# Recurrent attention and a two-way maxout layer: attention output in 64-column tiles, copied in the order it lies, token order restored by the stores

## The chip, the cores and the metric

The kernel runs on one core of one Trainium2 chip. The metric is the device time of one execution in microseconds. Times are told as medians of a few runs; a profiled execution, taken by the hardware profiler, gives the trace that the rows below come from. PE is the matrix engine (PEld its weight loads), DVE, ACT and POOL are the vector, scalar and general engines, and SP issues every DMA of this kernel, in the order of the program. Each core has 16 DMA engines, which share the packets of a transfer.

## What is computed

A recurrent attention over 768 tokens, for 4 batches and 8 heads of 48 columns, is followed by a layer that takes the larger of two products and multiplies once more:

```python
for t in range(S):
    cur = einsum('bhd,bhe->bhde', u[None] * kt, vt)
    y[:, :, t] = einsum('bhd,bhde->bhe', rt, state + cur)
    state = wt[:, :, :, None] * state + einsum('bhd,bhe->bhde', kt, vt)
x = y.transpose(0, 2, 1, 3).reshape(B * S, H * D)      # 3072 x 384
out = np.maximum(x @ w1, x @ w2) @ w_out               # d_ff 1024, out 3072 x 384
```

## The kernel before

Tokens go in segments of 256. A unit (`UNITS`) is one or two batches of one segment: the first four units hold one batch each of segment 0, the other four two batches each of segments 1 and 2. In a unit a token is numbered 2g + i: g runs over 128 partitions when the inputs are loaded (`load`, L357), and i over the two neighbours. After that g is split in two halves q of 64.

The text `ORDER` lists every step by name, unit and part, and the program is written out in that order; each engine runs its own share of it in that order, held by semaphores alone. There is no other scheduler. `name@a`, `@d`, `@p` put a step on ACT, DVE or POOL.

The steps that the change touches come at the end of a unit:

- `yi` (L654) adds the part of the output that comes from the state: for a head pair p and a half q, the weights are 128 rows (two heads of 64) by 96 columns (two heads of 48) of the state copy `S_b`, the moving operand is 128 tokens of `rT`. The output has heads' columns on partitions: pair p starts at row 96p of a 384-row range that is folded into blocks of 128 partitions.
- `ya` (L666) adds the part within a segment: for each head, 64 rows of masked scores `M` and 64 columns of `vp` (48 of them are the head's, the other 16 zero, so that the head's piece begins at a multiple of 32). It is called once per batch and neighbour j (in the first unit also once per half of the heads).
- `into` (L645) says which rows of the PSUM tile `Y` a matmul writes, and whether it is the first to write them; it keeps a set of the 32-row bands begun.
- `xe` (L678) copies `Y` to `xT` in bf16, on ACT for ten of twelve calls and on DVE for two.
- `gt` (L684) and `rl` (L696) multiply `xT` by the difference of the two first weights and keep the positive part in `gT`; `op` (L705) multiplies `xT` by a folded weight (L709) and `gT` by the last one (L713), with 128 tokens as the output's partitions.
- `oe` (L716) copies the 128 x 384 result to one of four `osb` buffers, and `os` (L721) stores it: 24 stores of 128 rows of 1,536 bytes, issued by SP between the loads and the transposes by DMA (`dt`, L566) of later units.

`Y` lies as q, block, i, g: the two neighbours i are 64 columns apart. Before, `xe` interleaves them, so that `xT`'s columns are tokens in their order, and the stores write 128 consecutive rows.

Of the kernel before, what the change touches and what calls it, by code (L numbers as in the profile page):

```python
# [114 lines left out]
def _body(tc, r, k, v, w, u, moe_w1, moe_w2, moe_w_out, out):  # L115
    nc = tc.nc
    B, H, S, D = r.shape
    P = 128
    Q = P // 2
    HD = H * D  # L120
    d_ff = moe_w1.shape[1]
    KO = HD // P
    FO = d_ff // P
    NP = H // 2
    DP = 64
# [11 lines left out]
    def wt_(shape, dt, tag, bufs=1):  # L137
        return wk.tile(shape, dt, tag=tag, name=tag, bufs=bufs)
# [19 lines left out]
    S_b = const.tile([P, 2, B, NP, 2, D], BF16)  # L158
# [6 lines left out]
    def copy(e, o, i):  # L165
        (nc.scalar.copy if e == "a" else nc.vector.tensor_copy if e == "d" else nc.gpsimd.tensor_copy)(  # L166
            o, i)
# [472 lines left out]
    def ytile(s, b):  # L640
        if b not in s.y:
            s.y[b] = pair()
        return s.y[b]

    def into(s, b, q, r0, n, i=None):  # L645

        o, c = r0 % P, r0 // P * P
        new = not all((b, q, x) in s.begun for x in range(o, o + n, 32))
        s.begun |= {(b, q, x) for x in range(o, o + n, 32)}
        y = ytile(s, b)[o:o + n, q, c:c + P].rearrange("c (i g) -> c i g", i=2)  # L650
        return dict(out=y if i is None else y[:, i, :], start=new, stop=False,
                    skip_group_check=True)

    def yi(s, b):  # L654
        for p in range(NP):
            for q in range(2):
                if s.c == 0 and q == 0:
                    continue
                for m in range(3):
                    nc.tensor.matmul(  # L660
                        lhsT=S_b[:, q, s.b0 + b, p].rearrange("d e c -> d (e c)")[
                            :, m * 32:(m + 1) * 32],
                        rhs=s.rT[:, b, :, p, q, :],
                        **into(s, b, q, p * 96 + m * 32, 32))

    def ya(s, b, j, y):  # L666
        n = NP // s.np
        for e in range(2):
            for p in range(y * n, (y + 1) * n):
                for m in range(2):  # L670
                    for q in range(2):
                        g = slice(q * Q, (q + 1) * Q)
                        nc.tensor.matmul(  # L673
                            lhsT=s.vp[g, b, 2 * p + e, j, m * 32:(m + 1) * 32],
                            rhs=s.M[b, j][g, :, 2 * p + e, :],
                            **into(s, b, q, p * 96 + (e + m) * 32, 32))

    def xe(s, b, e):  # L678
        if not hasattr(s, "xT"):
            s.xT = wt_([P, 4, KO, P], BF16, "xT", 2)  # L680
        copy(e, s.xT[:, 2 * b:2 * b + 2].rearrange("c q k (g i) -> c q k i g", i=2),
             s.y[b][:, :, 0:HD].rearrange("c q (k i g) -> c q k i g", i=2, k=KO))

    def gt(s, f):  # L684
        t = bank(F32, "G")
# [35 lines left out]
    def os(s, a):  # L721
        t = getattr(s, f"os{a}")
        t0 = (s.b0 + a // 2) * S + s.t0 + (a % 2) * P
        nc.sync.dma_start(out=out[t0:t0 + P, :], in_=t)

    ops = {"tri": c_tri, "tri2": c_tri2, "ident": c_ident, "mask": c_mask, "zero": c_zero, "u": dma_u,
           "wload": w_load, "woload": wo_load, "wdiff": w_diff, "hot": hot, "identb": c_identb, "identq": c_identq,
# [4 lines left out]
            "we": we, "rk": rk, "ru": ru, "dg": dg, "dd": dd, "di": di, "rw": rw, "kw": kw, "vb": vb,  # L732
            "scale": scale, "tr": tr, "te": te, "kv": kv, "st": st, "sm": sm, "sb": sb, "sc": sc,
            "mk": mk, "yi": yi, "ya": ya, "xe": xe, "gt": gt, "rl": rl, "op": op,
            "oe": oe, "os": os, "load": load, "dt": dt, "hi": hi, "lo": lo}
    for o in ORDER:
        o, _, e = o.partition("@")
        name, *a = o.split(".")
        a = [int(x) if x.isdigit() else x for x in a] + ([e] if e else [])
# [39 lines left out]
```

## Time and profile before

| what | value |
|---|---|
| median of 3 runs | 152.26 us (150.28 to 152.46) |
| profiled execution, its own time | 152.13 us |
| its span, from the first to the last instruction | 150.3 us |
| PE busy in the span | 92% |
| DVE / ACT / POOL busy | 79% / 61% / 60% |
| mean granted clock of PE | 0.974 |
| DMA queue of SP, share of 16 engines | 79.7% |
| the 24 stores, median from issue to landing | 2.5 us |

A row of a group reads: line, engine, operation, out<-in, partitions x elements and type, count, then busy us, mean ns of one, and the engine's idle time before it with what ended it. Matmuls overlap, so a group's busy time is the union of its records and is far below count times mean.

### The profile page before, as it was taken

The page shows a single profiled execution, that of the slowest core. Times are in us where ns is not written, and L with a number is a line of the kernel's source. Part 1 is how long each engine was busy: PE and PEld are TensorE (multiplying, and loading weights), DVE is VectorE, ACT ScalarE, POOL GpSimd, SP SyncE. Part 2 cuts the span into 40 slices and gives each one's busy share as a digit, 9 for nine tenths or more (in the row PEclk, how much of TensorE's full clock was granted, in tenths as well). Part 3 has the DMA queues.
Part 4 walks back from the last instruction along what each step waited for, and adds up shares of the span by engine and source line. Part 5 has one row for each costly group of instructions (what it writes and reads, how often), then busy time and mean ns, then how long its engine had stood idle before and what let it go on. Part 6 is the DMA issues. An engine that isn't in the chain of part 4 may idle for free.

```text
span 150.3 us, 5551 instructions
## 1 busy us (share of the span) xinstructions
PE 138.8 (92%) x2404; PEld 84.3 (56%) x2404; DVE 118.5 (79%) x161; ACT 91.6 (61%) x168; POOL 89.8 (60%) x102
## 2 busy tenths in 40 slices
PE   4779997799899998999999999999999999999991
PEld 1344645475676666764766546564667455664550
DVE  4593697999999999939999969796899887836510
ACT  3255463959989985995897785638736465033011
POOL 7878449796290779289999499590499900000000
PEclk9975899999999999999999999999999999999998
DMA  4999995999998959999993999679976693034042
GB/s 112 279 268 344 338 314 201 326 313 291 320 285 203 284 131 268 323 239 272 248 256 95 183 257 283 190 59 261 228 186 190 107 193 90 4 108 160 0 161 105
DMA packets 71187, 31.85 MB, mean 212 GB/s; under 512 B 66293, under 2 KB 70390, under 8 KB 71162
## 3 DMA queue, kind: packets, MB, share of 16 engines
q1 hardware_dynamic: 71162, 31.49, 79.7%
q8 instruction: 19, 0.31, 0.9%
q14 instruction: 6, 0.05, 0.1%
HBM read 23.61 MB, written 4.73 MB: 189 GB/s over the span
## 4 chain that ended last, share of the span: by engine, by line
PE 56%; DVE 18%; DMA 7%; POOL 6%; issue 5%; ACT 3%; SPq 3%; DVEq 0%; POOLq 0%; ACTq 0%
PE G L713 17%; PE G L691 16%; PE G L709 7%; DMA lr<-in_r_dram 7%; PE Y L673 4%; DVE M L635 3%; PE Y L626 3%; PE Y L660 2%; DVE dg L487 2%; PE G L232 2%; DVE rku L174 2%; SPq L357 2%; DVE kp L174 2%; DVE wst L398 2%; DVE rp L174 2%
## 5 line engine op out<-in xcount | busy, mean ns | idle before, releaser
L713 PE MATMUL G<-wo_sb,gT 128*128 128x384 bf16 x192 | 35.3, 326 | 0.1
L691 PE MATMUL G<-xT,wd_sb 128*128 128x256 bf16 (+1 forms) x192 | 34.1, 326 | 0.7 <-ACT xT L166 0.7
L635 DVE CAST_PREDICATED M<-mask,Y 128x1024 bf16<-128x1024 int32 (+1 forms) x26 | 28.9, 1136 | 4.1 <-PE Y L626 4.0
L701 ACT ACTIVATE gT<-G 128x512 bf16<-128x512 f32 x37 | 21.0, 603 | 11.1 <-PE G L691 11.0
L713 PEld LDWEIGHTS <-gT 128*128 128x128 bf16 x192 | 18.7, 98 | 12.9 <-ACT gT L701 0.7
L691 PEld LDWEIGHTS <-wd_sb 128*128 128x128 bf16 x192 | 18.2, 98 | 13.0 <-DVE M L501 0.7
L178 POOL TENSOR_TENSOR kp<-lk,iE 128x384 bf16<-128x384 f32 x16 | 18.2, 1163 | 3.0 <-ACT iE L445 2.2
L166 ACT COPY osb<-G 128x384 f32<-128x384 f32 x17 | 8.0, 481 | 14.2 <-PE G L713 13.4
L232 PE MATMUL G<-S_b 128*128 128x512 bf16 x48 | 14.8, 463 | 2.1 <-DVE S_b L261 2.1
L178 POOL TENSOR_TENSOR rku<-rku,u_b 128x384 f32<-128x384 f32 x14 | 14.1, 1029 | 3.2 <-DVE rku L174 2.0
L709 PE MATMUL G<-wc_sb,xT 128*128 128x384 bf16 x72 | 15.7, 328 | 0.0
L166 ACT CAST xT<-Y 128x768 bf16<-128x768 f32 x10 | 10.1, 1021 | 9.1 <-PE Y L660 7.5
L166 ACT COPY RK<-G 128x1024 bf16<-128x1024 bf16 x12 | 11.8, 1024 | 0.8 <-PE G L550 0.8
L487 DVE TENSOR_REDUCE dg<-rku 128x16 f32<-128x768 f32 x12 | 11.0, 945 | 0.0
L174 DVE TENSOR_TENSOR rp<-lr,G 128x768 bf16<-128x768 f32 (+2 forms) x13 | 10.5, 822 | 0.4 <-POOL rku L178 0.2
L425 DVE TENSOR_TENSOR MZ<-G,lg 128x384 f32<-128x384 f32 (+1 forms) x13 | 6.7, 521 | 5.3 <-PE G L383 4.6
L166 ACT CAST S_b<-S_f 64x192 bf16<-64x192 f32 (+1 forms) x16 | 9.4, 589 | 1.8 <-DVE S_f L597 1.6
L703 DVE TENSOR_SCALAR gT<-G 128x512 bf16<-128x512 f32 x11 | 7.4, 690 | 3.8 <-PE G L691 3.8
L232 PEld LDWEIGHTS <-S_b 128*128 128x128 bf16 x48 | 5.0, 114 | 9.6 <-issue 4.4
L174 DVE TENSOR_TENSOR rku<-lr,lk 128x768 f32<-128x768 f32 x9 | 9.7, 1092 | 0.0
L178 POOL TENSOR_TENSOR lk<-lk,lw 128x384 f32<-128x384 f32 x6 | 7.0, 1175 | 4.6 <-DVE rku L174 4.6
L673 PE MATMUL Y<-M,vp 64*32 64x128 bf16 x768 | 9.1, 219 | 0.4 <-DVE M L635 0.4
(101 smaller groups left out, 238.2 us busy)
## 6 DMA issues: line engine op xcount, KB each, us to landing
lk<-in_k_dram SPq DMA_DIRECT2D x12, 384.0 KB, 6.2
lr<-in_r_dram SPq DMA_DIRECT2D x12, 384.0 KB, 6.2
lv<-in_v_dram SPq DMA_DIRECT2D x12, 384.0 KB, 6.6
out_dram<-osb SPq DMA_DIRECT2D x24, 192.0 KB, 2.5
lw<-in_w_dram SPq DMA_DIRECT2D x11, 384.0 KB, 5.0
gT<-in_moe_w_dram SPq DMA_DIRECT2D x4, 512.0 KB, 6.4
wso<-in_moe_w_out_dram SPq DMA_DIRECT2D x4, 384.0 KB, 5.3
wst<-in_moe_w_dram SPq DMA_DIRECT2D x2, 512.0 KB, 5.9
```

The costliest lines, as they stand in the source:

```text
L166: (nc.scalar.copy if e == "a" else nc.vector.tensor_copy if e == "d" else nc.gpsimd.tensor_copy)(o, i)
L174: op(o, a, b)
L178: op(o[:, g], a[:, g], b[:, g])
L232: nc.tensor.matmul(t, zz[:, 0:P], zz[:, 0:512], start=True, stop=True)
L487: nc.vector.reduce_sum(s.dg[:, b].rearrange("p i h -> p h i"), s.rku[:, b], axis=AX.X)
L635: nc.vector.copy_predicated(t[:, :, 2 * n * y:2 * n * (y + 1)].rearrange("s i (p e) g -> s p e i g", e=2), mask[:, j].bitcast(I32).unsquee ...
L673: nc.tensor.matmul(lhsT=s.vp[g, b, 2 * p + e, j, m * 32:(m + 1) * 32], rhs=s.M[b, j][g, :, 2 * p + e, :], **into(s, b, q, p * 96 + (e + m) ...
L691: nc.tensor.matmul(t[:, m * n * P:(m + 1) * n * P].rearrange("c (b t) -> c b t", t=P), wd_sb[:, ko, fo * P:(fo + 1) * P], s.xT[:, 0:n, ko, :],
L701: nc.scalar.activation(o, i, AF.Relu)
L703: nc.vector.tensor_scalar_max(o, i, 0.0)
L709: nc.tensor.matmul(t[:, 0:HD], s.xT[:, a, ko, :], wc_sb[:, ko, :], start=(ko == 0), stop=False)
L713: nc.tensor.matmul(t[:, 0:HD], s.gT[:, c:c + P], wo_sb[:, f, :], start=False, stop=(f == FO - 1))
```

## The change

Three things are changed; `ORDER` is the same.

`yi` cuts the 96 columns of a pair in 64 + 32 (even pairs) or 32 + 64 (odd pairs), where it cut them in three tiles of 32. `ya` takes heads whose piece begins at a multiple of 64 rows as one tile of 64 columns (heads 0, 3, 4 and 7, sorted so that neighbours in order write different halves of the partitions), and the other four heads as two tiles of 32 each, as before. `into` asserts that the bands of one tile are all begun or all new.

`xe` copies `Y` to `xT` in the order in which it lies, so that `xT`'s columns are tokens in the order i, g. The output rows of `op` then have that order too, and `os` stores partition 64i + g to row 2g + i.

```diff
     def into(s, b, q, r0, n, i=None):
-        new = not all((b, q, x) in s.begun for x in range(o, o + n, 32))
+        old = [(b, q, x) in s.begun for x in range(o, o + n, 32)]
+        assert all(old) or not any(old)
+        new = not any(old)
 ...
-                for m in range(3):
+                for a, n in ((0, 64), (64, 32)) if p % 2 == 0 else ((0, 32), (32, 64)):
                     nc.tensor.matmul(
-                        lhsT=S_b[:, q, s.b0 + b, p].rearrange("d e c -> d (e c)")[
-                            :, m * 32:(m + 1) * 32],
+                        lhsT=S_b[:, q, s.b0 + b, p].rearrange("d e c -> d (e c)")[:, a:a + n],
                         rhs=s.rT[:, b, :, p, q, :],
-                        **into(s, b, q, p * 96 + m * 32, 32))
+                        **into(s, b, q, p * 96 + a, n))

     def ya(s, b, j, y):
         n = NP // s.np
-        for e in range(2):
-            for p in range(y * n, (y + 1) * n):
-                for m in range(2):
-                    for q in range(2):
-                        g = slice(q * Q, (q + 1) * Q)
-                        nc.tensor.matmul(
-                            lhsT=s.vp[g, b, 2 * p + e, j, m * 32:(m + 1) * 32],
-                            rhs=s.M[b, j][g, :, 2 * p + e, :],
-                            **into(s, b, q, p * 96 + (e + m) * 32, 32))
+        own = [2 * p + e for p in range(y * n, (y + 1) * n) for e in range(2)]
+        whole = [h for h in own if (h // 2 * 96 + h % 2 * 32) % DP == 0]
+        whole.sort(key=lambda h: (h // 2 % 2, h // 4))
+        parts_ = [h for h in own if h not in whole]
+        for h, w_ in [(h, DP) for h in whole] + [(h, 32) for h in parts_]:
+            for a in range(0, DP, w_):
+                for q in range(2):
+                    g = slice(q * Q, (q + 1) * Q)
+                    nc.tensor.matmul(
+                        lhsT=s.vp[g, b, h, j, a:a + w_],
+                        rhs=s.M[b, j][g, :, h, :],
+                        **into(s, b, q, h // 2 * 96 + h % 2 * 32 + a, w_))

     def xe(s, b, e):
-        copy(e, s.xT[:, 2 * b:2 * b + 2].rearrange("c q k (g i) -> c q k i g", i=2),
-             s.y[b][:, :, 0:HD].rearrange("c q (k i g) -> c q k i g", i=2, k=KO))
+        copy(e, s.xT[:, 2 * b:2 * b + 2].rearrange("c q k t -> c q (k t)"), s.y[b][:, :, 0:HD])

     def os(s, a):
-        nc.sync.dma_start(out=out[t0:t0 + P, :], in_=t)
+        nc.sync.dma_start(out=out[t0:t0 + P, :].rearrange("(g i) n -> i g n", i=2), in_=t)
```

What stands in the program now is shown at two places; a line with - is of before, one with + of the change. On SP, the stores among the transposes by DMA and the loads of the last units (`osb` is the buffer of `os`, `RK` the destination of `dt`, the shape is that of the destination):

```order
 L357 DMA lr<-in_r_dram 128x8x96 x2
 L567 DMA_TRANSPOSE RK<-rp_73 128x8x128
 L567 DMA_TRANSPOSE RK<-kp_75 128x8x128 x2
-L724 DMA out_dram<-osb 128x384
+L727 DMA out_dram<-osb 2x64x384
 L567 DMA_TRANSPOSE RK<-rp_73 128x8x128
-L724 DMA out_dram<-osb 128x384 x2
+L727 DMA out_dram<-osb 2x64x384 x2
 L357 DMA lw<-in_w_dram 128x8x96 x2
```

No transfer has moved; each of the 24 stores has a destination of three dimensions, the first of size 2, with rows two apart in it, where it had 128 consecutive rows.

On PE, the end of the first `yi` of the program as it was, and the beginning of the same `yi` as it is (the shape is that of the output, columns of the weights by tokens):

```order
-L660 LDWEIGHTS S_b
-L660 MATMUL Y<-RK,S_b 32x128
+L662 LDWEIGHTS S_b
+L662 MATMUL Y<-RK,S_b 64x128
+L662 LDWEIGHTS S_b
+L662 MATMUL Y<-RK,S_b 32x128
+L662 LDWEIGHTS S_b
+L662 MATMUL Y<-RK,S_b 32x128
+L662 LDWEIGHTS S_b
+L662 MATMUL Y<-RK,S_b 64x128
```

The block stands where it stood, with eight matmuls for twelve, and widths of 64 and 32 follow each other in it; in units with two halves q the widths alternate within a pair (64, 32, 64, 32, then 32, 64, 32, 64). `ya` has its matmuls of 64 columns first and those of 32 behind them.

## The prediction

> **What bounds the kernel now.** I read the page's head first, then the chain that ended last, then the DMA part and stretches of the DMA engines. The head says that PE and the DMA engines are both nearly full:
>
> ```profile
> span 150.3 us, 5551 instructions
> PE 138.8 (92%) x2404; PEld 84.3 (56%) x2404; DVE 118.5 (79%) x161; ACT 91.6 (61%) x168; POOL 89.8 (60%) x102
> PE   4779997799899998999999999999999999999991
> DMA  4999995999998959999993999679976693034042
> DMA packets 71187, 31.85 MB, mean 212 GB/s; under 512 B 66293, under 2 KB 70390, under 8 KB 71162
> q1 hardware_dynamic: 71162, 31.49, 79.7%
> PE 56%; DVE 18%; DMA 7%; POOL 6%; issue 5%; ACT 3%; SPq 3%; DVEq 0%; POOLq 0%; ACTq 0%
> ```
>
> The chain, in order of time (start us, us, what), shows where PE is the bound:
>
> ```profile
> 66.65 1.27 DVE wst L398
> 67.92 0.04 issue
> 67.96 0.32 PE G L381
> ...
> 75.23 0.35 PE Y L673 x32
> 75.59 0.79 PE Y L660 x48
> 76.38 0.59 PE G L709 x3
> 76.97 1.32 PE G L713 x8
> 78.29 0.49 PE G L709 x3
> ...
> 145.80 1.31 PE G L713 x8
> ...
> 147.18 0.48 ACT osb L166
> ```
>
> Until 68 us it runs through DVE, POOL and loads; from 67.96 it is almost all PE, up to the last copy out of PSUM at 147.18 and the last store. Shorter work in `ya` (L673) and `yi` (L660) would therefore count. But 79.7% over 16 DMA engines is 119.8 us of work on each, in a 150.3 us span: there is room for 30 us more per engine and no further. The change touches the stores, so this is the second resource to price.
>
> **The stores.** The issues (KB each, median us to landing), and three stretches (columns: stretch and its length, busy us of PE, PEld, DVE, ACT, POOL, granted clock, DMA share, GB/s):
>
> ```profile
> lk<-in_k_dram SPq DMA_DIRECT2D x12, 384.0 KB, 6.2
> out_dram<-osb SPq DMA_DIRECT2D x24, 192.0 KB, 2.5
> gT<-in_moe_w_dram SPq DMA_DIRECT2D x4, 512.0 KB, 6.4
> wst<-in_moe_w_dram SPq DMA_DIRECT2D x2, 512.0 KB, 5.9
> row<-MZ SPq DMA_DIRECT2D x2, 2.0 KB
> row<-MZ SPq DMA_DIRECT2D x2, 4.0 KB
> ...
> 148.50:148.80 0.30, 0.00 (x0) 0.00 (x0) 0.00 (x0) 0.00 (x0) 0.00 (x0) 1.00 0.91 348
> ...
> 59.50:68.00 8.50, 7.66 (x188) 5.60 (x186) 6.20 (x10) 7.94 (x14) 5.04 (x5) 1.00 1.04 285
> ...
> 56.00:150.30 94.30, 89.60 (x1721) 53.80 (x1719) 72.00 (x89) 54.01 (x93) 51.34 (x47) 0.99 0.72 178
> ```
>
> From 148.50 only the last store is in flight. It fills 0.91 of all 16 engines at 348 GB/s, so one busy engine moves 348 / (16 x 0.91) = 23.9 GB/s. A store of 196,608 B costs each of 16 engines 0.51 us.
>
> In the changed program the store's destination leads with a dimension of 2 (2x64x384) where source and destination both led with 128. How many engines share such a transfer? No transfer of this trace leads with 2. All that lead with 128 are spread over 16, as the stretch shows. Those that lead with 1 aren't cut at all: between 2 KB and 8 KB there are 71162 - 70390 = 772 packets, and 6 x 128 = 768 are the 4 KB rows of the six 512 KB weight loads (`gT`, `wst`); the other 4 are the four `row` copies, one packet each, so on one engine each. Both agree with shares cut along the leading dimension, as many as it allows. The bounds for a store are then 16 engines (0.51 us) and one (8.2 us); I take two, since equal shares along 2 and 128 can be cut no finer than in two: 98,304 B at 23.9 GB/s = **4.11 us on each of two engines**, eight times the time, on queues that every load also uses.
>
> The Trainium skill, "DMA: Bandwidth & Descriptors", section "Why a DMA increments its semaphore by 16 and not by 1", speaks against this change outright: the engines used are the largest number up to 16 that divides the sizes of both patterns' slowest dimension other than 1. By that rule it is 2, and the sum below stands; by an even spread, as of every store here, it would be the first rival's. No run here shows a leading 2 yet.
>
> **The sum.** SP issues all transfers in order (start us, us, engine, line, transfer):
>
> ```profile
> 54.77 1.70 SPq L357 DMA_DIRECT2D lr<-in_r_dram  x2
> 56.52 1.29 SPq L724 DMA_DIRECT2D out_dram<-osb  x1
> ...
> 75.43 1.19 SPq L357 DMA_DIRECT2D lr<-in_r_dram  x2
> 81.56 1.42 SPq L567 DMA_TRANSPOSE RK<-rp  x1
> ...
> 109.25 1.71 SPq L357 DMA_DIRECT2D lv<-in_v_dram  x2
> 111.05 2.65 SPq L724 DMA_DIRECT2D out_dram<-osb  x1
> ...
> 123.55 24.46 SPq L724 DMA_DIRECT2D out_dram<-osb  x11
> ...
> DMA to landing us min/median/max: 1.8/2.5/5.9
> ```
>
> (The last line is that of the stores.) From 56 us each engine has 0.72 x 94.3 = 67.9 us of work, 24 x 0.51 = 12.3 of it stores, so 55.6 us of other transfers. That share counts packets stretched by crowding (it passes 1.00 in the second stretch). From below, by bytes: 178 GB/s x 94.3 us - 4.7 MB = 12.1 MB, 754 KB per engine, at the second stretch's 285/16 = 17.8 GB/s, is 42 us. I take 48: two engines that are late while 14 idle are less crowded, but the transposes have smaller packets than those loads.
>
> So the two engines have 24 x 4.11 = 98.7 plus 48 = 147 us to do after the first store at 56.5, where PE needs 91 us. Do they ever rest? Up to the transposes of 81.56 they get four stores and fourteen loads, from the two of 54.77 to the two of 75.43: 16.4 + 14 x 1.38 (24.6 KB each at 17.8 GB/s) = 36 us, to some 93 us, so the next work comes well before. Later PE yields 24 outputs in 91 us, one per 3.8, and the two engines take 6.1 per output. At the end, the 12 stores of the last two rows stand behind the last `lv`, 49 us of moving against 38 us of PE work. I add nothing for rest.
>
> The fixed part of a store is its fastest landing, 1.8, less 0.6 of moving: 1.2. The last copy ends at 147.18 + 0.48 = 147.7; 1.8 later, at 149.5, its store has landed, and the span had 0.8 left. The span becomes 56.5 + 1.2 + 98.7 + 48 + 0.8 = 205.2. The profiled execution took 152.13 against its span of 150.3, so 1.8 lies around it; it is 0.1% below the median of the runs shown, 152.26. **Forecast: 207 us.**
>
> What waits in turn: `load` and `dt` transfers stand behind stores in the two engines' queues and are complete only when these two are. `oe` has four `osb` buffers, so a copy waits for the store four before it; it sits on ACT (or DVE) ahead of later `rl` copies, for which PE's L713 waits. All PE savings are then hidden.
>
> **What PE and ACT save**, where they count:
>
> ```profile
> L691 PE MATMUL G<-xT,wd_sb 128*128 128x256 bf16 (+1 forms) x192 | 34.1, 326 | 0.7 <-ACT xT L166 0.7
> L701 ACT ACTIVATE gT<-G 128x512 bf16<-128x512 f32 x37 | 21.0, 603 | 11.1 <-PE G L691 11.0
> L166 ACT COPY osb<-G 128x384 f32<-128x384 f32 x17 | 8.0, 481 | 14.2 <-PE G L713 13.4
> L166 ACT CAST xT<-Y 128x768 bf16<-128x768 f32 x10 | 10.1, 1021 | 9.1 <-PE Y L660 7.5
> L673 PE MATMUL Y<-M,vp 64*32 64x128 bf16 x768 | 9.1, 219 | 0.4 <-DVE M L635 0.4
> ```
>
> `ya` goes from 768 matmuls to 576. The chain gives 0.35 us for 32, 10.9 ns each; at that rate 24 take 0.26, and 24 such blocks save 2.1 us. From the other side, if time goes by columns rather than by instruction, nothing is saved, since 64 columns are as many as two tiles of 32. I take 2.1, as 10.9 is well below the 16.5 of `yi` and looks set by issue. `yi` goes from 240 to 160: 48 take 0.79, so 0 to -1.3; I take -0.6. `xe` writes in order instead of alternating: by the copies of 384 and 512 columns (481 and 603, 0.95 ns a column) 768 would take 847 ns, 0.17 less; PE's wait for `xT` is 0.7 in all, so 0 to -0.7, taken as -0.3. Together -3.0.
>
> **Rivals.** (1) *Spread over 16 engines stays*, because the queue divides by rows and not by the leading dimension: 152.1 - 3.0 = **149.1**, on the border of 2%, which is about what a measurement of this kernel can tell from no change. For it: 128 rows of 1,536 B remain, as before. Against it: the one-packet `row` copies. It decides as soon as a store uses nine engines or more: then it adds under 0.4 us to each, inside the 30 us of room.
>
> (2) *Spread stays, but a change of tile width empties the array.* `yi` now changes width 4 times in a block of the first four units and 12 in the eight others, 112 in all, and `ya` once in each of 26 calls. The three matmuls of L709 take 0.59 us behind `yi`'s narrow tiles and 0.49 behind L713's full ones: at most 0.10 us a change, and nothing from below. 138 changes x 0.10 = 13.8, so 152.1 - 3.0 + 13.8 = **163**; from 0.02 us a change the gain is gone. Against it: that 0.10 may lie in the weights, and changes between neighbours in other columns may overlap.
> The Trainium skill, "TensorEngine Tiling (Array Packing)", section "Key Properties", says that changing the mode drains TensorE; by that rule this rival comes true wherever the first would, and under the forecast it is covered.
>
> (3) *One engine*: 24 x 8.2 = 197 in place of 98.7: **306**.
>
> **How the numbers follow.** Two engines 0.84; rival one 0.07 (0.03 faster, 0.04 the same); rival two 0.04; rival three 0.03; something between, such as four engines, 0.02 (half of it counted as the same). The forecast's ends: others 42 and packets a tenth faster without the crowd give 56.5 + 1.2 + 89 + 42 + 0.8 + 1.8 = 191; others 55.6 and 12 us of rest give 227. The range is 188 to 228 and leaves out some 0.2, nearly all of it the other cases.
>
> **What would show it.** Right: the last stores land 4 us apart; for the last 30 us the DMA share is near 2/16 = 0.12 at some 48 GB/s; the stores' median landing rises from 2.5 to over 8 and the loads' from 6.2; the chain names DMA, and PE's share of the span falls below 70%. The packet count stays. Wrong: 1.8 us landings at the end (rival one or two; then L662 against 0.79 for 48 tells which). If two engines alone ran their packets much faster than 23.9 GB/s, the size would be off and not the mechanism.

## The result and the profile after

The changed kernel takes 207.53 us (median; 206.28 to 207.74) against 151.4 us (150.28 to 152.46) of the kernel before: 1.368 times as long, 95% interval 1.359 to 1.377. Times here are medians of all executions of a kernel, while ratios leave out those that ran over 1.5% longer than the fastest of the same kernel; the profiled executions of two runs below, the new tiles with split stores (179.18 us) and the leading 8 (155.19 us), are such longer ones and are read for single stretches only. The forecast was 207 us. The experiments show that the mechanism is the forecast's, and that the closeness of the number owes something to two errors that cancel.

The changed kernel's head, slices, queue, chain shares and three groups, and then the group of `yi` in the kernel before (its `ya`, L673, stands in the prediction):

```profile
span 205.6 us, 5007 instructions
PE 168.3 (82%) x2132; PEld 96.7 (47%) x2132; DVE 118.1 (57%) x161; ACT 90.1 (44%) x168; POOL 88.4 (43%) x102
PEclk9859999999999997599969999755599999995555
DMA  5999699999584698477854797153982011111110
GB/s 138 287 331 344 239 341 295 324 241 246 145 228 119 186 269 221 100 142 142 91 143 136 156 216 135 45 154 89 107 117 65 18 45 47 50 50 50 50 50 35
q1 hardware_dynamic: 70826, 31.49, 61.8%
PE 30%; DMA 24%; POOL 10%; ACT 9%; issue 7%; SPq 6%; DVE 5%; ACTq 0%; POOLq 0%; DVEq 0%
L662 PE MATMUL Y<-RK,S_b 128*64 128x128 bf16 (+1 forms) x160 | 23.1, 253 | 0.0
L166 ACT CAST xT<-Y 128x768 bf16<-128x768 f32 x10 | 8.0, 799 | 22.9 <-PE Y L662 12.4 <-PE Y L677 10.4
L677 PE MATMUL Y<-M,vp 64*32 64x128 bf16 (+1 forms) x576 | 13.8, 237 | 0.0
```

```profile
L660 PE MATMUL Y<-RK,S_b 128*32 128x128 bf16 x240 | 5.1, 221 | 0.0
```

Two things stand out. The last eight slices move 45 to 50 GB/s (35 in the very last) at a DMA share of about a tenth, which is what two engines of 16 would give. And `yi` (L662) is busy 23.1 us with 160 matmuls, where 240 took 5.1 before; `ya` (L677) takes 13.8 with 576, where 768 took 9.1. PE is busy longer with fewer instructions.

The end of the time in three stretches (stretch, length, busy us of PE, PEld, DVE, ACT, POOL, granted clock, DMA share, GB/s):

```profile
158.00:163.00 5.00, 5.00 (x143) 2.85 (x142) 4.14 (x6) 0.00 (x0) 0.00 (x0) 1.00 0.06 22
163.00:170.00 7.00, 7.00 (x63) 4.04 (x64) 0.96 (x1) 1.28 (x2) 0.00 (x0) 1.00 0.13 43
170.00:203.00 33.00, 11.79 (x65) 6.16 (x63) 5.08 (x8) 2.53 (x5) 0.00 (x0) 0.74 0.13 50
```

2/16 is 0.125. For 33 us two engines move 50 GB/s, 25 each, and PE works a third of the time. A store of 196,608 B takes them 3.93 us. From 158 to 163 even these two have little to do: PE is full, and no result is ready to be stored.

Who waited for whom (us in total, times, longest), and the chain (start us, us, what):

```profile
ACT osb L166 <- DMA out_dram<-osb: 23.8, 4, 8.2
...
DVE osb L166 <- DMA out_dram<-osb: 16.2, 3, 6.4
```

```profile
76.65 0.47 PE Y L677 x24
77.12 4.71 PE Y L662 x31
81.83 1.07 PE G L712 x3
82.91 2.56 PE G L716 x8
...
163.22 4.19 PE Y L662 x32
...
170.41 10.86 DMA out_dram<-osb
...
181.87 7.22 DMA out_dram<-osb
...
189.19 0.48 ACT osb L166
```

The `osb` copies wait 40 us for stores. In the kernel before, the same view had this line alone for them:

```profile
ACT osb L166 <- DMA out_dram<-osb: 0.8, 1, 0.8
```

In the chain `yi` is seen at 4.71 and 4.19 us for a unit of two batches, where 48 matmuls took 0.79 before. Behind the one at 77.12, L712 takes 1.07 us (0.59 before, behind `yi`) and L716 2.56 (1.32 before). PE is busy there without a gap, but the granted clock is half:

```profile
80.00:86.00 6.00, 6.00 (x24) 2.87 (x25) 0.50 (x2) 1.71 (x3) 4.48 (x5) 0.50 0.50 117
```

Behind the one at 163.22 the clock stays at 1.00, as the second stretch above shows.

### The profile page after: what moved, and what is told of

It is laid out like the page before. It is cut to its first block, busy times and chain, and to the rows that moved or that the text cites. A ratio compares the mean times of both kernels' runs of the same rounds, so it can differ in the third digit from the quotient of the medians.

```text
span 205.6 us, 5007 instructions
## 1 busy us (share of the span) xinstructions
PE 168.3 (82%) x2132; PEld 96.7 (47%) x2132; DVE 118.1 (57%) x161; ACT 90.1 (44%) x168; POOL 88.4 (43%) x102
## 4 chain that ended last, share of the span: by engine, by line
PE 30%; DMA 24%; POOL 10%; ACT 9%; issue 7%; SPq 6%; DVE 5%; ACTq 0%; POOLq 0%; DVEq 0%
DMA out_dram<-osb 12%; DMA lw<-in_w_dram 8%; PE G L716 8%; PE Y L662 8%; PE G L694 6%; PE G L712 3%; PE Y L677 3%; ACT gT L704 3%; SPq L357 3%; POOL kp L178 2%; DMA lr<-in_r_dram 2%; DMA wso<-in_moe_w_out_dram 2%; DVE rku L174 2%; POOL lg L178 1%; SPq L288 1%
## 5 line engine op out<-in xcount | busy, mean ns | idle before, releaser
L716 PE MATMUL G<-wo_sb,gT 128*128 128x384 bf16 x192 | 40.3, 358 | 0.1
L716 PEld LDWEIGHTS <-gT 128*128 128x128 bf16 x192 | 20.6, 107 | 16.6 <-issue 5.9
L662 PE MATMUL Y<-RK,S_b 128*64 128x128 bf16 (+1 forms) x160 | 23.1, 253 | 0.0
L712 PE MATMUL G<-wc_sb,xT 128*128 128x384 bf16 x72 | 18.2, 367 | 4.1 <-ACT osb L166 4.1
L166 ACT CAST xT<-Y 128x768 bf16<-128x768 f32 x10 | 8.0, 799 | 22.9 <-PE Y L662 12.4
L662 PEld LDWEIGHTS <-S_b 128*64 128x64 bf16 (+1 forms) x160 | 12.7, 103 | 10.7 <-issue 0.6
L166 DVE COPY osb<-G 128x384 f32<-128x384 f32 x7 | 3.8, 555 | 23.0 <-DMA out_dram<-osb 16.2
L677 PE MATMUL Y<-M,vp 64*32 64x128 bf16 (+1 forms) x576 | 13.8, 237 | 0.0
L677 PEld LDWEIGHTS <-vp 64*32 64x32 bf16 (+1 forms) x576 | 7.5, 97 | 8.0 <-issue 4.7
L626 PE MATMUL Y<-RK 48*64 48x128 bf16 x384 | 9.4, 224 | 2.0 <-DMA RK<-rp 2.0
```

The costliest lines, as they stand in the source:

```text
L626: nc.tensor.matmul(t[q * Q:(q + 1) * Q, e, p * P:(p + 1) * P].rearrange("s (i g) -> s i g", i=2), s.kT[d, b, j, y * n + p, q, :], s.rT[d, ...
L662: nc.tensor.matmul(lhsT=S_b[:, q, s.b0 + b, p].rearrange("d e c -> d (e c)")[:, a:a + n], rhs=s.rT[:, b, :, p, q, :], **into(s, b, q, p * ...
L677: nc.tensor.matmul(lhsT=s.vp[g, b, h, j, a:a + w_], rhs=s.M[b, j][g, :, h, :], **into(s, b, q, h // 2 * 96 + h % 2 * 32 + a, w_))
L712: nc.tensor.matmul(t[:, 0:HD], s.xT[:, a, ko, :], wc_sb[:, ko, :], start=(ko == 0), stop=False)
L716: nc.tensor.matmul(t[:, 0:HD], s.gT[:, c:c + P], wo_sb[:, f, :], start=False, stop=(f == FO - 1))
```

## The experiments

The questions: do the stores alone make the time, or do the matmuls of changing width? Is it the leading dimension that sets the number of engines, or rows that aren't neighbours, or the third dimension?

**Old tiles, two engines.** `yi` and `ya` as before; the rest is the change:

```diff
-                for a, n in ((0, 64), (64, 32)) if p % 2 == 0 else ((0, 32), (32, 64)):
+                for m in range(3):
 ...
-        for h, w_ in [(h, DP) for h in whole] + [(h, 32) for h in parts_]:
+        for e in range(2):
+            for p in range(y * n, (y + 1) * n):
```

> The change with yi and ya as they were before (tiles of 32 columns); the copy xe in order and the stores with the leading 2 stay. Theory (two DMA engines carry all stores and set the end): 24 x 4.11 us of stores and some 48 us of other transfers on two engines follow the first store at 56.5, whatever PE does, so 200 to 207 us, as with the change. Rival (the matmuls of changing width set the time: L662 takes 4.2 us for 32 at full clock in the changed kernel's trace, where 48 took 0.79): taking them away gives back the 18 to 19 us that they added, 186 to 190 us. Between 191 and 199: both bind in turn.

Measured: 202.14 us, 1.328 times the kernel before (1.315 to 1.340). Its chain and three stretches:

```profile
DMA 37%; DVE 13%; PE 13%; SPq 10%; POOL 9%; ACT 5%; issue 5%; ACTq 0%; DVEq 0%; POOLq 0%
DMA out_dram<-osb 27%; PE G L692 6%; SPq L357 5%; SPq L567 4%; DMA lr<-in_r_dram 4%; POOL rku L178 4%; DVE M L635 3%; DMA lw<-in_w_dram 3%; DMA RK<-rp 2%; DVE rku L174 2%; ACT RK L166 1%; DVE M L501 1%; DVE rp L174 1%; DVE dg L487 1%; PE G L714 1%
```

```profile
152.00:156.00 4.00, 3.52 (x159) 2.27 (x148) 3.29 (x4) 0.00 (x0) 0.00 (x0) 1.00 0.12 42
156.00:164.00 8.00, 4.86 (x78) 2.65 (x69) 2.43 (x4) 1.28 (x2) 0.00 (x0) 0.99 0.14 45
164.00:196.00 32.00, 12.87 (x59) 6.27 (x58) 3.75 (x6) 2.53 (x5) 0.00 (x0) 0.66 0.13 49
```

The two engines are full from 152 on without the gap that the changed kernel has at 158 to 163. So the stores, with the copy in order, make the time some 50 us longer. (A run further below has the same old tiles and the same copy, with stores spread over 16 engines: it takes 155.3 us, so the 50 us are not the copy's.) The tiles add 5.4 us on top, much less than the 21 us by which they lengthen PE's busy time (168.3 against 147.1).

**New tiles, stores over 16 engines.** Each store becomes two transfers of 64 rows, whose patterns lead with 64:

```diff
-        nc.sync.dma_start(out=out[t0:t0 + P, :].rearrange("(g i) n -> i g n", i=2), in_=t)
+        for i in range(2):
+            nc.sync.dma_start(out=out[t0:t0 + P, :].rearrange("(g i) n -> i g n", i=2)[i],
+                              in_=t[i * Q:(i + 1) * Q])
```

> The change, but each store cut in two transfers of 64 rows (even and odd rows), whose patterns lead with 64. Theory: these spread over 16 engines, the store costs each engine half a microsecond again, PE is the bound, and what is left is the cost of changing widths: yi 4 x 0.85 + 8 x 2.1 us = 20.2 against 4.3 before, ya 24 x 0.12 = 2.9 more, so 18.8 us more on PE, of which some 2 us lie before 68 us beside other work: 166 to 170 us. Rival (the stores have no part in it, two engines or not, for instance because rows two apart are slow to write): stays at 203 to 210 us. Rival (the widths cost nothing once the stores are quick): 149 to 152 us.

Measured: 174.65 us, 1.144 times (1.133 to 1.156); above the expected 166 to 170, and far from both rivals. Its chain, and two stretches:

```profile
148.57 1.89 PE Y L677 x96
150.46 4.71 PE Y L662 x32
155.17 1.07 PE G L712 x3
156.24 2.56 PE G L716 x8
158.80 5.84 PE G L694 x24
164.64 0.49 PE G L712 x3
```

```profile
146.00:151.00 5.00, 5.00 (x145) 3.00 (x144) 3.37 (x5) 0.00 (x0) 0.00 (x0) 1.00 0.08 19
151.00:158.00 7.00, 7.00 (x39) 3.61 (x38) 0.96 (x1) 0.80 (x1) 0.00 (x0) 0.66 0.18 46
```

PE is recorded busy throughout, but the granted clock, still 1.00 at 152, is 0.50 from about 153, inside the block of 32 matmuls, to 160 (0.66 is the mean of the stretch). In that time matmuls take twice as long: L716 2.56 us for 1.30. The expectation had the widths' direct price right and counted nothing for this second one, nor for the split of the stores itself, which a run below puts at 3 us.

Not every such block does this. The three traces with the changed kernel's order in `yi` (its own, this run's, and that of the run with only `yi` new below) hold eight blocks of 32 that begin at full clock. The clock fell in four of them, for 3.4 to 6.8 us, and in the other four it stayed at 1.00. The Trainium skill, "TensorE: Matmul & The Clock Gate", section "What's actually happening", says that the clock follows how busy PE has recently been. The changed kernel's trace agrees where PE is recorded idle: PE is idle from 128.6 to 131, and from 131.6 to 136 the clock is 0.50. For the blocks it would fit only if a PE that changes width counts as little busy although its records show no idle time; no run shows that directly.

**Leading dimension 4, 16 and 8**, each one edit to the kernel before:

```diff
-        nc.sync.dma_start(out=out[t0:t0 + P, :], in_=t)
+        nc.sync.dma_start(out=out[t0:t0 + P, :].rearrange("(g a) n -> a g n", a=4), in_=t)
```

> The kernel before with one edit: the store's destination leads with 4 (partition 32a + g goes to row 4g + a), so the rows of the output stand in another order within each 128; everything else as before. Theory (as many engines as the leading dimension): four engines, 2.06 us a store on each, 56.5 + 1.2 + 24 x 2.06 + 48 + 0.8 + 1.8 = 158 us. Rival (the spread goes by rows, and only the change's other parts cost time): 150 to 153 us.

> As the run with a leading 4, with 16 instead (partition 8a + g goes to row 16g + a): rows of the output in another order within each 128. Theory: 16 engines, nothing lost, 150 to 153 us, and the last stores land 1.8 us after their issue. Rival (rows that aren't neighbours in memory, or a third dimension in the pattern, are what costs): as slow as the run with a leading 4, or slower.

> The kernel before with a store whose destination leads with 8 (partition 16a + g goes to row 8g + a): the rows of the output stand in another order within each 128. By the sum of work, eight engines have 24 x 1.03 + 48 = 73 us to do after the first store, less than PE's 91, and the last store moves 0.5 us longer: 151 to 153.5 us. Rival (with a leading 4 the time was 168.8 where the sum gave 158, so it is not the sum alone: loads that stand behind a store come late even on an engine that has time to spare): 154 to 158 us.

Measured: 168.78 us with 4 (1.111 times, 1.100 to 1.122); 152.72 with 16 (1.001, 0.996 to 1.006); 154.26 with 8 (1.011, 0.999 to 1.023). Of the run with 4, a load in its chain, a wait, and a stretch at the end with only stores in flight; then the stores of the run with 16 (KB each, median us to landing), and of the run with 8 a stretch at the end, again with only stores in flight:

```profile
94.01 8.45 DMA lw<-in_w_dram
```

```profile
ACT osb L166 <- DMA out_dram<-osb: 14.2, 6, 5.1
```

```profile
161.70:165.70 4.00, 0.00 (x0) 0.00 (x0) 0.00 (x0) 0.00 (x0) 0.00 (x0) 0.50 0.26 95
```

```profile
out_dram<-osb SPq DMA_DIRECT2D x24, 192.0 KB, 2.8
```

```profile
151.30:151.90 0.60, 0.00 (x0) 0.00 (x0) 0.00 (x0) 0.00 (x0) 0.00 (x0) 1.00 0.48 174
```

Rows apart in memory and a third dimension cost no time that can be seen when 16 leads, although a single store lands later (median 2.8 us for 2.5, and the fastest 2.5 where the expectation had 1.8). In these stretches with only stores in flight, and from 192 to 204 in the changed kernel, the DMA share is 0.13 under a leading 2, 0.26 under 4 and 0.48 under 8: close to 2/16, 4/16 and 8/16. It is the leading dimension. The Trainium skill's rule ("DMA: Bandwidth & Descriptors", the section named in the prediction) holds here for 2, 4 and 8, and the time with 16 agrees with it.

But with 4 the time was 168.8 where the sum of work gave 158: four engines have some 97 us of work in 110 us of time. In that run's chain a load of `lw` takes 8.45 us, and the copies wait for `osb` again, 14.2 us on ACT in all. So it seems that single loads come late before the engines are full; no run tests that alone. With 8 the interval holds both no change and a loss of 2%, so it decides neither for the expectation nor for its rival. Where a narrower spread begins to cost time lies between 16 and 4 and stays open.

**Split store and the copy in order, old tiles.**

```diff
-        copy(e, s.xT[:, 2 * b:2 * b + 2].rearrange("c q k (g i) -> c q k i g", i=2),
-             s.y[b][:, :, 0:HD].rearrange("c q (k i g) -> c q k i g", i=2, k=KO))
+        copy(e, s.xT[:, 2 * b:2 * b + 2].rearrange("c q k t -> c q (k t)"), s.y[b][:, :, 0:HD])
```

> The change without its matmul tiles and without its store: xe copies in order, yi and ya have tiles of 32 as before, each store is two transfers of 64 rows. Theory (stores over 16 engines and no change of width leave only the quicker copy): xe takes 799 ns for 1,021, PE waited 0.7 us for xT in all, and the last result needs a second issue of 0.4 us: 0.5 us less to 0.5 more than the kernel before. Rival (48 stores of half the size crowd SP's queue): 2 us or more slower.

Measured: 155.3 us, 1.019 times (1.011 to 1.028): some 3 us slower, so the rival holds. SP's last issues in this run and then in the kernel before, and this run's last copy:

```profile
144.69 6.23 SPq L726 DMA_DIRECT2D out_dram<-osb  x10
```

```profile
144.11 3.91 SPq L724 DMA_DIRECT2D out_dram<-osb  x5
```

```profile
147.76 0.48 ACT osb L166
```

Its span is 153.3 us, so it ends 5.1 us after the last copy; the kernel before ended 2.6 after its own. Some 2.5 of the 3 us lie behind the last copy, where ten transfers queue on SP.

**The split store issued by two engines.**

```diff
-            nc.sync.dma_start(out=out[t0:t0 + P, :].rearrange("(g i) n -> i g n", i=2)[i],
+            (nc.sync, nc.scalar)[i].dma_start(out=out[t0:t0 + P, :].rearrange("(g i) n -> i g n", i=2)[i],
```

> As the run with split stores and old tiles, with the even rows' transfer issued by SP and the odd rows' by ACT. Theory (that run's 3 us are SP's, which issues the last ten transfers in 6.23 us where five took 3.91, behind the last copies): the tail gets some 2 us shorter, 150.5 to 153.5 us. Rival (transfers of 64 rows are slow to land, or the other half comes from elsewhere): 154 us or more.

Measured: 155.87 us, 1.029 times (1.019 to 1.038): no gain.

```profile
ACT osb L166 <- DMA out_dram<-osb: 9.9, 6, 3.1
```

```profile
147.67 0.50 ACTq L726
148.17 0.04 issue
148.21 2.51 DMA out_dram<-osb
150.74 0.48 ACT osb L166
```

The issues on ACT stand between ACT's own copies, and these copies now wait 9.9 us for `osb` buffers, 3.0 in the run before; the last one starts 3 us later. What was gained behind the last copy was lost ahead of it; why the stores free the buffers later was not tested.

**Only `yi` new, and `yi` with the wide tiles first.** The first has `ya` as before, with split stores. The second does, in each block, all tiles of 64 and then all of 32:

```diff
+        wide = [(p, q, 0 if p % 2 == 0 else 32, 64) for p in (0, 2, 1, 3) for q in range(2)]
+        narrow = [(p, q, 64 if p % 2 == 0 else 0, 32) for q in range(2) for p in range(NP)]
+        for p, q, a, n in wide + narrow:
```

> The change with split stores and with ya as before, so that of the tiles only yi is new. Theory (each of 112 changes of width in yi costs 0.16 us: L662 took 23.1 us in the changed kernel's trace against 5.05 for L660 before): 16 to 18 us on PE, some 2 of them hidden before 68 us, and up to 6 us of half clock behind the two-batch blocks; 166 to 172 us, 2 to 4 below the run with both. Rival (ya's widths cost as much, or the clock alone makes the loss): under 163 us.

> As the run with only yi new, but yi does all its tiles of 64 first and then all its tiles of 32: the same 160 matmuls with one change of width in a block, 12 in all, where there were 112. Theory (the change of width is what costs): 12 x 0.16 = 2 us, less what fewer matmuls save: 152 to 156 us, and the clock stays at 1.0 behind the blocks. Rival (tiles of 64 columns with 128 rows are slow in themselves, or fewer matmuls let the clock fall): 165 us or more.

Measured: 170.76 us (1.128 times, 1.120 to 1.136) and 155.75 us (1.028, 1.021 to 1.035). The group of `yi` and its first block of 32 matmuls (start us, us), first of the former and then of the latter:

```profile
L662 PE MATMUL Y<-RK,S_b 128*64 128x128 bf16 (+1 forms) x160 | 21.1, 237 | 0.0
77.85 4.26 PE L662 MATMUL Y<-RK,S_b 128*64 128x128 bf16 x32
```

```profile
L662 PE MATMUL Y<-RK,S_b 128*64 128x128 bf16 (+1 forms) x160 | 6.8, 226 | 0.0
74.37 1.22 PE L662 MATMUL Y<-RK,S_b 128*64 128x128 bf16 x32
```

The same 160 matmuls, with 112 changes of width or with 15 (one in each of the 12 calls, and one more in each of the three places where two calls follow each other directly, which the expectation left out): 14.3 us for 97 changes, 0.147 us each. And 15 us of time. Single blocks at full clock agree: 4.26 us against 1.22 for 32 matmuls is 0.145 a change for 21 changes, and 2.25 against 0.64 for 16 matmuls is 0.146 for 11. In the second run the clock stayed at 1.00 behind all three blocks of 32. It is level with the run that has old tiles and the same stores (155.3), so tiles of 64 neither gain nor lose visible time once they stand together. The Trainium skill, "TensorEngine Tiling (Array Packing)", section "Key Properties", says that a change of tiling mode drains TensorE; these runs agree and give it a price. `ya` is the difference of 174.65 to 170.76, 3.9 us, and its group is busy 12.9 us with the new tiles, 9.1 with the old. That is not a price of one change: where calls of `ya` follow each other the width changes back between them as well, and no run takes its tiles apart.

**A version meant to be faster**: tiles of 32, ordered so that neighbours write different columns.

```diff
     def yi(s, b):
+        for q in range(2):
 ...
+            for p in range(NP):
+                for m in range(3):
 ...
     def ya(s, b, j, y):
+        for h in whole + [h for h in own if h not in whole]:
+            for m in range(2):
                 for q in range(2):
```

> A version meant to be faster than both: tiles of 32 throughout, xe in order, stores split in two transfers of 64 rows; yi does one half q after the other, so that neighbours in order write different column groups, and ya takes its heads in the changed kernel's order (0, 4, 3, 7, then 1, 2, 5, 6) with tiles of 32. Theory (yi's 16.5 ns a matmul comes from waiting for the same columns, 13.3 would be four at once; ya's 10.9 may be issue): 0.6 to 0.9 us from yi, 0 to 3 from ya, 0 to 0.5 from xe: 148.5 to 152 us where the kernel before is at 152.9. Rival (both are bound by issue): no change.

Measured: 153.96 us, 1.019 times (1.011 to 1.026), with the split stores' loss in it. Its two groups:

```profile
L677 PE MATMUL Y<-M,vp 64*32 64x128 bf16 x768 | 9.1, 220 | 0.0
L662 PE MATMUL Y<-RK,S_b 128*32 128x128 bf16 x240 | 5.1, 221 | 0.0
```

Both are what they were, 9.1 and 5.1 us: this order of column groups changes nothing, and the rival holds. No run beat the kernel before.

## Why the prediction was right

*Two engines.* The step on which all rests held: 0.13 of the DMA engines and 50 GB/s to the end, the shares with 4 and 8, the time with 16, and 202 us with the new stores and the old tiles.

*4.11 us a store.* It was 3.93: two engines alone move 25 GB/s each, 23.9 were read from 16 that ran together. Over 24 stores that is 4.3 us too many.

*48 us of other transfers.* With 3.93 and its own first store at 54.3 us, the run with old tiles should take 54.3 + 1.2 + 94.4 + 48 + 0.8 + 1.8 = 200.5; its profiled execution took 200.72. So 48 with no rest fits, though nothing measured the two apart.

*"I add nothing for rest", "all PE savings are then hidden".* The first fits with old tiles and fails with the new ones. For the changed kernel, first store at 57.15, the same sum gives 203.4, and the profiled execution took 207.33. About 2.6 of the 4 us are the half-empty stretch from 158 to 163; the rest wasn't located. PE's part was not a saving to be hidden but a loss, and it showed twice: in the first store, 2.9 us later than in the run with old tiles, and in that stretch, where PE had no result ready for the two engines. The missing rest (about 4 us too few) and the size of a store (4.3 too many) cancel, so the closeness of the number was luck; without the second the forecast would have been off by 2%.

*What PE saves, -3.0 us.* Wrong in sign, and without weight under the forecast. `ya` at 10.9 ns a matmul was to take 0.26 us for 24 and took 0.47; `yi` went from 5.1 to 23.1 us busy. The -0.17 us for each copy of `xe` was right in kind: 799 ns for 1,021.

*Rival two, 163 us.* Had the stores stayed spread, it would have come true, and dearer: with the split stores the time is 174.65, of which some 3 us are the split itself. "At most 0.10 us a change" was read from one kind of change, from narrow tiles to full ones; a change between widths that follow each other costs 0.147, and the clock that falls in some of these blocks was no term at all. The rival's doubt, that changes between neighbours in other columns might overlap, is refuted: those of `yi` are such, and they cost this much.

*Rival one* did not come true, as the stores weren't spread. Its 149.1 would have failed even then: 174.65 with the new tiles, and 155.75 with `yi` alone new and its widths one after the other, some 3 us of each being the split.

*The signs.* The DMA share, the GB/s, DMA in the chain and the waits for `osb` came as told. "PE's share below 70%" did not: it is 82%, since the time of the width changes is recorded as busy; with old tiles it is 74%, still not below 70. Landing times of the stores and loads can't be read, as that view gives none for the changed kernel.

## What to carry to other kernels

Look at the leading dimension of a transfer's pattern before its row length: here a permutation on the memory side that led with 2 left 14 of 16 engines out, and what stood behind it in the queue waited too. Count how often neighbouring matmuls change their tile width, since that, and not the number of matmuls, set the time of `yi`; do the widths one after the other. A forecast that fits isn't proof of its terms: only running the parts apart showed two errors of 4 us that cancelled.

## What was not expected of the hardware

- A change of tile width between neighbouring matmuls with 128 rows cost 0.147 us (97 changes, 14.3 us), though the profile shows no idle PE.
- The granted clock fell to 0.50 in four of eight blocks of 32 such matmuls (4.2 to 4.7 us each), for 3.4 to 6.8 us, with PE recorded busy all the time; in three blocks with the widths one after the other it stayed at 1.00.
- The matmuls of `ya` and `yi` with tiles of 32 took 9.1 and 5.1 us in both orders that were tried.
- Ten transfers of 64 rows took SP 6.23 us to issue, five of 128 rows 3.91.
